# Routing tokens to experts: three fixed slots per expert and a table for the rest, in place of one table for all

## The chip, the core and the metric

The kernel runs on one core of one Trainium2 chip. A core has five engines with queues of their own: TensorE (PE, with its weight loads shown apart as PEld), VectorE (DVE), ScalarE (ACT), GpSimd (POOL) and SyncE (SP, which here only issues transfers). Sixteen DMA engines serve transfers that SP or POOL issue. The metric is the time of one execution on the device in microseconds (us), lower is better; kernels are compared by the median of their runs.

## The reference

Chunked attention over q, k, v of shape 4 x 8 x 768 x 64, with eight memory rows per head, gives 3072 tokens of 512 values. These go through a mixture of experts:

```python
h_dense = np.maximum(x @ w1_dense, 0.0)
y_dense = h_dense @ w2_dense
logits = x @ w_gate
expert_idx = np.argmax(logits, axis=1)
...
for e in range(E):
    mask = expert_idx == e
    h = np.maximum(x[mask] @ w1[e], 0.0)
    y_moe[mask] = gate_w[mask, None] * (h @ w2[e])
return (y_dense + y_moe).astype(np.float32)
```

There are E = 8 experts with weights of 512 x 512, twice each. `gate_w` is the softmax weight of the chosen expert. The inputs are drawn with a fixed seed, so how many tokens go to which expert is the same in every run: 339, 581, 96, 448, 352, 375, 288 and 593 for experts 0 to 7 (worked out by running the reference's attention and gate on its inputs).

## The kernel before, in words

**Attention stage.** The 3072 tokens are 24 tiles of 128. A loop written out by hand (`manual_schedule`, so the order of the code is the order on each engine) runs iterations 0 to 28, and in each of them different parts of several tiles: scores of tile i, values of tile i-2, the transposes of tile i-3, the gate of tile i-4, the dense first layer of tile i-7 (L363, its Relu in L365). SP issues the value windows (`load_v`, L182) and the gate's weights (`wgate`, L444, after the second window). POOL issues q and k (`load_qk`) and the expert weights (`load_w`, L83), one half of one expert at a time: 12 halves in the iterations of `W_AT`, one behind the loop, four more around the first slots. All weights end in one SBUF tile `wall`. Constants are set in iteration 0, among them a row `zrow` (L114 to L117) that says "no token".

**Routing.** Every third tile, `choose`, `rank` and `place` (DVE and PE) give each token of three tiles a row in a DRAM buffer `xs`, which has a region of 3072 rows per expert. `scatter` (L424, an indirect DMA of POOL) writes each token's row there: its values in bf16, its dense hidden values, its gate weight and its number. At the end `cnt` (L526) holds the tokens per expert.

**Table.** From `cnt`, some twenty small DVE operations (L541 to L582) build a table of 31 slots: for slot j its expert (`expi`) and the 128 row numbers of `xs` (`rowi`; lanes without a token point at the zero row).

**Slots.** Each slot handles 128 rows of one expert. `fetch` (L594) gathers the rows by an indirect DMA of POOL, `turn` (L602) transposes them on PE and copies the result out (half on DVE, half on ACT), `bring` (L612) reads the expert's number into a DVE register and copies that expert's weights out of `wall` by two DVE copies, `first` (L623) is the first layer (16 matmuls, L628), `second` (L634) the dense and the expert's second layer (four matmuls each), `send` (L646) scales on ACT and `put` (L655) stores by an indirect DMA of POOL to the tokens' rows of the output. `run` interleaves them: in slot n it brings slot n+1, runs its own first layer, the dense second layer, turns slot n+1, runs its own second layer, sends, and fetches four slots ahead. Slots 0 to 26 always run; four further slots run inside an If (L698) when the table has more than NSURE = 27 slots. Their fetches, and their stores of a zeroed tile, run in any case.

Of the kernel before, what the change touches and what calls it, by code (L numbers as in the profile page):

```python
# [17 lines left out]
ENGINES = [mybir.EngineType.PE, mybir.EngineType.DVE, mybir.EngineType.Activation]  # L18
# [17 lines left out]
NSLOT = NT + E - 1  # L36
NSURE = 27
NSPLIT = 20
XW = DM // 2
ROW = 2 * XW + 2  # L40
ZROW = E * CAP
NOWHERE = 1 << 20
GRP = 3
QKB = 5
NVB = 4
W_AT = (10, 13, 15, 16, 18, 19, 21, 22, 24, 25, 26, 27)
NXG = 5
# [3 lines left out]
def kernel(  # L51
# [19 lines left out]
    xs = nc.dram_tensor("xs", [E * CAP + 1, ROW], I32, kind="Internal").ap()  # L71
# [14 lines left out]
    w_todo = [(E, 1)] + [(e, half) for e in range(E) for half in range(2)]  # L86
# [12 lines left out]
    zrow = const.tile([1, ROW], F32, name="zrow")  # L99
    rowi = const.tile([128, NSLOT], I32, name="rowi")  # L100
    expi = const.tile([128, NSLOT], I32, name="expi")
    nsl = const.tile([128, 1], I32, name="nsl")
    thr_i = const.tile([128, NT], I32, name="thr_i")
    thr = const.tile([128, NT], F32, name="thr")
    lane_i = const.tile([128, 1], I32, name="lane_i")
    lane = const.tile([128, 1], F32, name="lane")
    slot_i = const.tile([128, NSLOT], I32, name="slot_i")
    slot = const.tile([128, NSLOT], F32, name="slot")
    low = const.tile([128, E, E], F32, name="low")

    def constants():
        nc.vector.memset(ones, 1.0)
        nc.vector.memset(oh_sum, 0.0)
        nc.vector.memset(zrow, 0.0)  # L114
        nc.vector.memset(zrow[:, ROW - 2:ROW - 1], 1.0)
        nc.vector.memset(zrow[:, ROW - 1:ROW].bitcast(I32), NOWHERE)
        nc.sync.dma_start(xs[ZROW:ZROW + 1, :], zrow.bitcast(I32))  # L117
        for e in range(E):
            nc.gpsimd.memset(prio[:, e:e + 1], float(E - e))
            nc.gpsimd.memset(ecap[:, :, e:e + 1], float(e * CAP // 128))  # L120
        nc.gpsimd.iota(tok, [[128, NT]], base=0, channel_multiplier=1)
        nc.gpsimd.affine_select(upper, ones, pattern=[[1, 128]], base=0,
                                channel_multiplier=-1, compare_op=ALU.is_gt, fill=0.0)

    def table_constants():
        nc.gpsimd.iota(thr_i, [[128, NT]], base=0, channel_multiplier=0)
        nc.gpsimd.iota(lane_i, [[0, 1]], base=0, channel_multiplier=1)
        nc.gpsimd.iota(slot_i, [[1, NSLOT]], base=0, channel_multiplier=0)
        nc.vector.tensor_copy(thr, thr_i)
        nc.vector.tensor_copy(lane, lane_i)  # L130
        nc.vector.tensor_copy(slot, slot_i)
        nc.vector.memset(low, 0.0)
# [3 lines left out]
    with ExitStack() as one:  # L136
# [4 lines left out]
        small = one.enter_context(tc.tile_pool(name="small", bufs=2))  # L141
        ps = one.enter_context(tc.tile_pool(name="ps", bufs=4, space=PSUM))
        px = one.enter_context(tc.tile_pool(name="px", bufs=1, space=PSUM))
        pf = one.enter_context(tc.tile_pool(name="pf", bufs=1, space=PSUM))
# [25 lines left out]
        vebuf = [c1.tile([128, HP, D + 1], F32, name=f"ve{n}") for n in range(2)]  # L170
        vws = {n: vbuf[n % NVB] for n in range(B * NP)}
        ves = {b: vebuf[b % 2] for b in range(B)}
# [102 lines left out]
        def attention(g, qT, kbd):  # L275
# [84 lines left out]
            def dense():  # L360
                ph = pf.tile([128, F], F32, tag="ph", name="ph")
                for d in range(DT):
                    nc.tensor.matmul(ph, st["xT"][:, d, :], wall[:, E, d, :],  # L363
                                     start=(d == 0), stop=(d == DT - 1))
                nc.scalar.activation(st["row"][:, XW:2 * XW].bitcast(BF16), ph, AF.Relu,  # L365
                                     scale=st["grp"]["gt"][:, st["u"], 0:1])

            return {"scores": scores, "exp": expo, "turn": turn, "values": values, "norm": norm,
                    "keep_x": keep_x, "turn_x": turn_x, "gate": gate, "dense": dense}

        scatters = []

        def wide(ap, n=GRP):
            return ap.unsqueeze(2).to_broadcast([128, n, E])

        def choose(grp):
            lg = grp["pg"]
            mx = small.tile([128, GRP], F32, tag="gmx", name="gmx")
            nc.vector.reduce_max(mx, lg, axis=AX.X)
            df = small.tile([128, GRP, E], F32, tag="df", name="df")  # L380
            nc.vector.tensor_tensor(df, lg, wide(mx), ALU.subtract)
            pr = small.tile([128, GRP, E], F32, tag="pr", name="pr")
            nc.vector.scalar_tensor_tensor(
                pr, df, 0.0, prio.unsqueeze(1).to_broadcast([128, GRP, E]),
                op0=ALU.is_ge, op1=ALU.mult)
            pm = small.tile([128, GRP], F32, tag="pm", name="pm")
            nc.vector.reduce_max(pm, pr, axis=AX.X)
            oh = small.tile([128, GRP, E], BF16, tag="oh", name="oh")
            nc.vector.tensor_tensor(oh, pr, wide(pm), ALU.is_equal)
            ex = small.tile([128, GRP, E], F32, tag="ex", name="ex")  # L390
# [3 lines left out]
        def weigh(grp):  # L394
            nc.vector.reduce_sum(grp["gt"][:, :, 0], grp["ex"], axis=AX.X)

        def rank(grp, last):
            oh = grp["oh"]
            rk = ps.tile([128, GRP, E], F32, tag="ps", name="rk")
            nc.tensor.matmul(rk, ones, ecap, start=True, stop=False)  # L400
            for t in range(GRP):
                nc.tensor.matmul(rk, ones, oh_sum[:, t:t + 1, :].to_broadcast([128, GRP, E]),
                                 start=False, stop=False)
            for t in range(GRP - 1):
                nc.tensor.matmul(rk[:, t + 1:, :], ones,
                                 oh[:, t:t + 1, :].to_broadcast([128, GRP - 1 - t, E]),
                                 start=False, stop=False)
            nc.tensor.matmul(rk, upper, oh, start=False, stop=True)
            (nc.vector if last else nc.gpsimd).tensor_tensor(oh_sum, oh_sum, oh, ALU.add)
            grp["rk"] = rk  # L410

        def place(grp):
            at = small.tile([128, GRP, E], F32, tag="at", name="at")
            nc.vector.tensor_tensor(at, grp["rk"], grp["oh"], ALU.mult)
            si = small.tile([128, GRP], I32, tag="si", name="si")
# [3 lines left out]

        def scatter(g):  # L420
            st = tiles.pop(g)
            grp, u, row = st["grp"], st["u"], st["row"]
            nc.gpsimd.tensor_copy(row[:, ROW - 2:], grp["gt"][:, u, :])  # L423
            i = nc.gpsimd.indirect_dma_start(  # L424
                xs[:, :], bass.IndirectOffsetOnAxis(ap=grp["si"][:, u:u + 1], axis=0),
                row.bitcast(I32), None, bounds_check=E * CAP - 1, oob_is_err=False)
            for o in scatters:
# [14 lines left out]
        make_identity(nc, identf)  # L442
        load_v(1)
        nc.sync.dma_start(wgate, moe_w_gate.rearrange("(t p) m -> p t m", p=128))  # L444
# [10 lines left out]
        parts, grps = {}, {}  # L455
        LAG_X, LAG_G, LAG_D = 3, 4, 7
        for i in range(NT + LAG_G + 1):
# [4 lines left out]
            if i < NT:  # L462
# [9 lines left out]
                if i % GRP == 0:  # L472
                    grps[i // GRP] = {}
                tiles[i]["grp"], tiles[i]["u"] = grps[i // GRP], i % GRP
            gg = i - LAG_G
            grp = grps[gg // GRP] if 0 <= gg < NT else None
            last = grp is not None and gg % GRP == GRP - 1
# [4 lines left out]
            if i == 2:  # L482
                load_w(E, 0)
                table_constants()
            if i in W_AT:
                next_w()
            if i % 2 == 0:
                load_v(i // 2 + 2)
            if grp is not None and gg % GRP == 0:
                grp["pg"] = pg.tile([128, GRP, E], F32, tag="pg", name="pg")  # L490
                grp["gt"] = small.tile([128, GRP, 2], F32, tag="gt", name="gt", bufs=3)
                nc.gpsimd.tensor_copy(grp["gt"][:, :, 1].bitcast(I32), tok[:, gg:gg + GRP])
# [8 lines left out]
            if i < NT + LAG_G:  # L501
                do("dense", LAG_D)
            else:
                for g in range(i - LAG_D, NT):
                    parts[g]["dense"]()
            do("gate", LAG_G)
# [9 lines left out]
            if last:  # L516
# [6 lines left out]
                weigh(grp)  # L523
                place(grp)
# [4 lines left out]
            if i >= LAG_D:  # L529
                scatter(i - LAG_D)  # L530
        for g in range(NT + LAG_G + 1 - LAG_D, NT):
            scatter(g)
        next_w()
# [6 lines left out]
        m24 = wide_t[1][:, :E * NT].rearrange("p (e t) -> p e t", t=NT)  # L540
        nc.vector.tensor_tensor(m24, cnt.unsqueeze(2).to_broadcast([128, E, NT]),  # L541
# [196 lines left out]
```

## Time and profile before

| what | value |
|---|---|
| median of three runs | 290.79 us (288.57 to 292.19) |
| the profiled execution, its own time | 287.78 us |
| its span, first to last instruction | 286.1 us |
| granted TensorE clock, mean | 0.921 |
| busy share: PE, DVE, ACT, POOL | 77%, 60%, 49%, 67% |
| DMA, mean over the span | 45.15 MB, 158 GB/s |
| idle of PE ahead of the turns, waiting for fetched rows | 25.6 us |

The profile comes from one execution. Times in it are microseconds from the span's start unless marked ns. A group's row gives line, engine, operation, output<-inputs and shape, then the count, busy time and mean duration of one in ns, and behind the second bar the idle time of the engine just before these instructions with what ended it. A row of the timeline gives start, duration, engine, line and count, and in brackets the idle before it. A row of the windows gives, for a stretch of time, the busy time of each engine, the granted clock, the DMA engines' busy share (which can pass 1 where packets overlap) and GB/s.

### The profile page before, as it was taken

Reading aid. Unit: us, or ns where it says so; the run is one execution under the profiler, and the core shown is the slowest. Engines: PE = TensorE matmul, PEld = TensorE weight load, DVE = VectorE, ACT = ScalarE, POOL = GpSimd, SP = SyncE. Lnnn points to the kernel's source line nnn. Section 1 sums busy time; section 2 is a strip of 40 time slices with the busy share of each in tenths; the row PEclk is TensorE's granted clock in tenths of the full one; section 3 lists DMA queues with packets and bytes.
Section 4 is the critical chain, followed back from the end, with each engine's and each line's share of the span. In section 5 each row is a group of like instructions: output and inputs, shape, how many; then the busy total and the mean of one; then the engine's idle time right before and its main releaser. Section 6 shows DMA issues by size and latency. Waiting matters only on the chain. (4 is left out here: it accounts for less than half of the span.)

```text
span 286.1 us, 9435 instructions
## 1 busy us (share of the span) xinstructions
PE 219.7 (77%) x3770; PEld 163.6 (57%) x3804; DVE 173.0 (60%) x384; ACT 140.9 (49%) x230; POOL 190.5 (67%) x274
## 2 busy tenths in 40 slices
PE   2435759999879969998997202997999999865691
PEld 1324658877767857867775002664666667534460
DVE  5586356888768967988974711464556656552230
ACT  2434446776976767653553200353546656441341
POOL 8864034599958984885879807365676877887732
PEclk9999977999999997999999855797999999995979
DMA  6999546599998999699969995994455555454231
GB/s 88 179 200 172 109 84 93 101 174 166 170 234 134 212 218 221 96 210 223 200 129 177 204 165 123 193 230 141 139 158 158 183 153 173 152 162 131 84 112 60
DMA packets 54368, 45.15 MB, mean 158 GB/s; under 512 B 30319, under 2 KB 49263, under 8 KB 54322
## 3 DMA queue, kind: packets, MB, share of 16 engines
q0 software_dynamic: 25376, 36.54, 62.1%
q1 hardware_dynamic: 28946, 7.98, 15.2%
q8 instruction: 31, 0.51, 0.8%
q14 instruction: 15, 0.12, 0.1%
HBM read 46.05 MB, written 14.44 MB: 211 GB/s over the span
## 5 line engine op out<-in xcount | busy, mean ns | idle before, releaser
L596 POOL DMA_INDIRECT xg<-xs,rowi x31 | 36.6, 1180 | 24.3 <-issue 13.1
L609 ACT COPY xT<-xt 128x512 bf16<-128x512 bf16 x27 | 15.8, 586 | 59.9 <-DVE xT L608 59.9
L608 DVE COPY xT<-xt 128x512 bf16<-128x512 bf16 x27 | 11.5, 425 | 50.6 <-PE xt L606 50.6
L656 POOL DMA_INDIRECT out_dram<-o,xg x27 | 28.1, 1039 | 18.7 <-ACT o L651 9.0
L606 PE MATMUL xt<-ident,xg 128*128 128x128 bf16 x216 | 18.2, 233 | 25.6 <-DMA xg<-xs,rowi 25.6
L628 PEld LDWEIGHTS <-wa 128*128 128x128 bf16 x432 | 29.2, 105 | 9.0 <-issue 2.3
L606 PEld LDWEIGHTS <-xg 128*128 128x128 bf16 x216 | 15.0, 104 | 33.8 <-DMA xg<-xs,rowi 29.4
L424 POOL DMA_INDIRECT xs<-row,si x24 | 29.6, 1233 | 6.8 <-POOL row L423 6.5
L628 PE MATMUL ph<-xT,wa 128*128 128x128 bf16 x432 | 31.5, 231 | 1.5 <-ACTq L698 1.0
L351 POOL CAST xT<-x 128x512 bf16<-128x512 f32 x24 | 15.0, 626 | 25.0 <-ACT x L349 21.7
L643 PE MATMUL py<-wb,h 128*128 128x512 bf16 x108 | 30.8, 412 | 0.0
L357 PEld LDWEIGHTS pg<-wgate,x 128*128 128x128 f32 x192 | 26.1, 199 | 5.9 <-ACT qT L257 2.4
L322 PE MATMUL xp<-vw,aT 64*32 64x65 f32 x1536 | 25.6, 233 | 4.9 <-DMA vw<-mtpl 3.0
L223 DVE COPY vw<-vw 24x1820 f32<-24x1820 f32 x24 | 27.5, 1147 | 2.5 <-DMA vw<-in_v_dram 1.8
L363 PE MATMUL ph<-wall,xT 128*128 128x512 bf16 x76 | 23.5, 390 | 5.8 <-issue 2.1
L341 POOL CAST row<-xn 128x512 bf16<-128x512 f32 x24 | 19.5, 814 | 11.6 <-DVE xn L334 11.4
L617 DVE COPY wa<-wall 128x2048 bf16 (+1 forms) x27 | 20.4, 755 | 11.3 <-DVE gw L648 7.6
L305 ACT ACTIVATE a<-a 128x512 f32<-128x512 f32 x24 | 15.1, 630 | 24.0 <-DVE a L300 22.5
L640 PE MATMUL py<-wall,xT 128*128 128x512 bf16 x94 | 25.6, 388 | 0.9 <-issue 0.2
L357 PE MATMUL pg<-wgate,x 128*128 128x8 f32 x192 | 24.4, 253 | 2.3 <-DMA wgate<-in_moe_w_gate_dram 2.3
L322 PEld LDWEIGHTS xp<-vw,aT 64*32 64x32 f32 x1536 | 19.2, 109 | 11.7 <-issue 5.6
L265 ACT COPY kbd<-tp 64x768 bf16<-64x768 bf16 x28 | 22.1, 790 | 3.4 <-PE tp L252 3.2
(122 smaller groups left out, 449.4 us busy)
## 6 DMA issues: line engine op xcount, KB each, us to landing
wall<-in_moe_w_dram POOLq DMA_DIRECT2D x16, 512.0 KB, 9.2
vw<-in_v_dram SPq DMA_DIRECT2D x64, 64.0 KB
kb<-in_k_dram POOLq DMA_DIRECT2D x16, 192.0 KB, 6.0
qb<-in_q_dram POOLq DMA_DIRECT2D x16, 192.0 KB, 6.9
vw<-in_v_dram SPq DMA_DIRECT2D x32, 56.0 KB
vw<-mtpl SPq DMA_DIRECT2D x24, 65.0 KB
wall<-in_moe_w_dense_dram POOLq DMA_DIRECT2D x2, 512.0 KB, 8.5
xg<-xs,rowi POOLq DMA_INDIRECT x31, 4.2
```

The lines of the kernel that those rows point to most:

```text
L223: nc.vector.tensor_copy(vw[r + 32:r + 56, :PC - 1], vw[r:r + 24, 1:])
L265: nc.scalar.copy(dst, tv[r])
L322: nc.tensor.matmul(xp[32 * cc:32 * cc + 32, par, (D + 1) * hp:(D + 1) * (hp + 1)], st["aT"][r, hp, 32 * cc:32 * cc + 32], vw[r, 4 * (g % 2 ...
L357: nc.tensor.matmul(grp["pg"][:, u, :], st["x32"][:, d, :], wgate[:, d, :], start=(d == 0), stop=(d == DT - 1))
L363: nc.tensor.matmul(ph, st["xT"][:, d, :], wall[:, E, d, :], start=(d == 0), stop=(d == DT - 1))
L424: i = nc.gpsimd.indirect_dma_start(xs[:, :], bass.IndirectOffsetOnAxis(ap=grp["si"][:, u:u + 1], axis=0), row.bitcast(I32), None, bounds_c ...
L596: nc.gpsimd.indirect_dma_start(xg.bitcast(I32), None, xs[:, :], bass.IndirectOffsetOnAxis(ap=rowi[:, j:j + 1], axis=0), bounds_check=ZROW, ...
L606: nc.tensor.transpose(xt[:, d, :], xb[:, 128 * d:128 * d + 128], ident)
L628: nc.tensor.matmul(ph[:, f, :], w[:, d, 128 * f:128 * f + 128], xT[:, d, :], start=(d == 0), stop=(d == DT - 1))
L640: nc.tensor.matmul(py, xts[j][:, DT + f, :], wall[:, E, DT + f, :], start=(f == 0), stop=False)
L643: nc.tensor.matmul(py, hs[j][:, f, :], copied[j][1][:, f, :], start=False, stop=(f == FT - 1))
L656: i = nc.gpsimd.indirect_dma_start(out[:, :], bass.IndirectOffsetOnAxis(ap=xgs.pop(j)[:, ROW - 1:ROW].bitcast(I32), axis=0), o, None, boun ...
```

## The change

Every expert gets three fixed slots (FIX = 3, 24 in all, slots 0 to 23); slot j uses expert j // 3, with its weights read in `wall` where they lie. Tokens beyond 384 of an expert go to table slots: three of these (SURE = 3, slots 24 to 26) run always, the other 18 (slots 27 to 44) in an If that is entered when the table needs more than three. Table slots still copy their weights. A slot's 128 rows are now contiguous in `xs`: each region of `xs` starts with 128 filler rows, and a slot that is not full ends at the expert's last row, so that it also reads rows of the slot before, or filler. A lane that is not the slot's own is masked by `past`, which sends its store out of range. SP reads the start row into a register and issues a plain DMA.

Weights: expert 0, the dense second layer and expert 1 are loaded in the attention stage (iterations 12, 15, 17, 19, 21), the other twelve halves in the slots of `W_SLOT`. The attention loop has one iteration less; the last dense tiles run behind the last gate, in other PSUM buffers. Value windows have five buffers and are loaded one window further ahead; `wgate` goes ahead of the second window. Eight transfers of SP write the filler rows (`front`). 36 matmuls whose result is not used stand ahead of the first turn.

```diff
-NSLOT = NT + E - 1
-NSURE = 27
-NSPLIT = 20
+FIX = 3
+NFIX = FIX * E
+NOVER = NT - FIX
+SURE = 3
+REG = CAP + 128
...
-QKB = 5
-NVB = 4
-W_AT = (10, 13, 15, 16, 18, 19, 21, 22, 24, 25, 26, 27)
-NXG = 5
+GROUPS = [GRP] * 7 + [2, 1]
+QKB = 4
+NVB = 5
+W_AT = (12, 15, 17, 19, 21)
+W_SLOT = (0, 1, 3, 4, 6, 7, 9, 10, 12, 13, 15, 16)
+NXG = 6
+NIDLE = 36
...
-    w_todo = [(E, 1)] + [(e, half) for e in range(E) for half in range(2)]
+    w_todo = [(0, 0), (0, 1), (E, 1)] + [(e, half) for e in range(1, E) for half in range(2)]
...
-        nc.vector.memset(zrow, 0.0)
...
-        nc.sync.dma_start(xs[ZROW:ZROW + 1, :], zrow.bitcast(I32))
+        nc.vector.memset(wall[:, E - 1], 1.0)
...
+    def front(e):
+        i = nc.sync.dma_start(
+            xs[REG * e:REG * e + 128, :],
+            wall[:, E - 1].rearrange("p t m -> p (t m)")[:, :2 * ROW].bitcast(I32))
...
+        nc.sync.dma_start(wgate, moe_w_gate.rearrange("(t p) m -> p t m", p=128))
         load_v(1)
-        nc.sync.dma_start(wgate, moe_w_gate.rearrange("(t p) m -> p t m", p=128))
...
+        send_at = {i: [i - 7] for i in range(7, 25)}
+        send_at.update({25: [18], 26: [19, 20], 27: [21]})
+        dense_at = {i: [i - 7] for i in range(7, 25)}
+        dense_at.update({25: [18, 19], 26: [20], 27: [21, 22, 23]})
...
-            if i % 2 == 0:
-                load_v(i // 2 + 2)
+            if 3 <= i < 3 + E:
+                front(i - 3)
+            if i < 2:
+                load_v(i + 2)
+            elif i % 2 == 0:
+                load_v(i // 2 + 3)
...
+        rs = tmp(FS, "rsf")
+        nc.vector.tensor_tensor(rs, full, cnt.unsqueeze(2).to_broadcast(FS), ALU.min)
+        nc.vector.tensor_tensor(by_slot(rowi), rs, base, ALU.add)
+        nc.vector.tensor_tensor(rs, full, rs, ALU.subtract)
+        nc.vector.tensor_scalar(by_slot(past), rs, lane, float(NOWHERE),
+                                op0=ALU.is_gt, op1=ALU.mult)
...
         def fetch(j):
-            xg = w3.tile([128, ROW], F32, tag="xg" + own[0], name="xg", bufs=NXG)
-            nc.gpsimd.indirect_dma_start(
-                xg.bitcast(I32), None, xs[:, :],
-                bass.IndirectOffsetOnAxis(ap=rowi[:, j:j + 1], axis=0),
-                bounds_check=ZROW, oob_is_err=True)
+            at = nc.sync.value_load(rowi[:1, j:j + 1], min_val=0, max_val=E * REG - 128)
+            xg = w3.tile([128, ROW], F32, tag="xg", name="xg", bufs=NXG)
+            nc.sync.dma_start(xg.bitcast(I32), xs[bass.ds(at, 128), :])
...
         def bring(j):
+            if j < NFIX:
+                w = wall[:, j // FIX]
+                was[j] = w[:, :DT], w[:, DT:]
+                return
+            k = j - NFIX
+            ev = nc.vector.value_load(expi[:1, k:k + 1], min_val=0, max_val=E - 1)
...
+            to = w3.tile([128, 1], I32, tag="to", name="to")
+            nc.vector.tensor_scalar(to, xg[:, ROW - 1:ROW].bitcast(I32), past[:, j:j + 1],
+                                    float(NOWHERE), op0=ALU.max, op1=ALU.min)
...
+        sure = list(range(NFIX + SURE))
+        more = list(range(NFIX + SURE, NSLOT))
+        for j in sure[:NXG]:
             fetch(j)
         bring(0)
+        idle = pf.tile([128, DM], F32, tag="py", name="idle")
+        for n in range(NIDLE):
+            nc.tensor.matmul(idle, ident, wall[:, E, n % DT], start=True, stop=True)
         turn(0)
...
+        run(sure)
+        count = nc.values_load(nov[:1, :1], min_val=0, max_val=NOVER)
+        with tc.If(count > SURE, preferred_fallthrough_block=False):
+            for j in more[:NXG]:
+                fetch(j)
             bring(more[0])
             turn(more[0])
+            run(more)
```

In `run`, the fetch now goes NXG = 6 slots ahead, and nothing outside the given list of slots is brought, turned or fetched.

289 lines of the change are left out of this document (146 added, 143 removed).

## The prediction

> **What bounds the kernel now.** I read the windows by stage first, then the timeline of the slots for their pace, then the groups by line and the waits for the stalls in them. The attention stage ends near 163 us; a gap without TensorE work follows; from 176 us on the routed tiles ("slots") run.
>
> ```profile
> 163.00:178.00 15.00, 1.20 (x10) 0.93 (x11) 1.90 (x4) 0.14 (x1) 5.63 (x7) 0.50 0.77 155
> 176.20:183.35 7.15, 6.33 (x39) 4.41 (x41) 2.94 (x6) 1.75 (x3) 3.81 (x5) 0.53 0.90 187
> 183.35:192.34 8.99, 8.94 (x96) 6.20 (x96) 5.46 (x12) 4.85 (x9) 5.04 (x5) 1.00 1.16 217
> 192.34:198.94 6.60, 4.56 (x33) 2.67 (x33) 2.59 (x7) 2.36 (x4) 3.13 (x4) 0.82 0.49 137
> 198.94:246.74 47.80, 46.46 (x474) 32.05 (x480) 26.94 (x61) 27.29 (x46) 35.81 (x32) 0.99 0.53 165
> ```
>
> Columns: stretch, length, busy time of PE, PEld, DVE, ACT, POOL, granted clock, DMA share, GB/s. In the fifth row PE is busy 46.46 of 47.80 us at clock 0.99: an undisturbed slot is TensorE-bound. Its pace, from the output copies (eleven slots apart), and the number of slots:
>
> ```profile
> 212.22 0.69 ACT L651 ACTIVATE o<-py,gw 128x512 f32<-128x512 f32 x1
> 245.95 0.69 ACT L651 ACTIVATE o<-py,gw 128x512 f32<-128x512 f32 x1
> L628 PE MATMUL ph<-xT,wa 128*128 128x128 bf16 x432 | 31.5, 231 | 1.5 <-ACTq L698 1.0 <-DVE xT L608 0.5
> ```
>
> 33.73 / 11 = 3.07 us a slot, and 432 matmuls of 16 a slot are 27 slots: the four spare ones in the If of before are skipped. From the first of these matmuls (177.84) to the last of the span (280.12) are 102.3 us; 27 x 3.07 is 82.9. The other 19.4 are a cold start and late fetches:
>
> ```profile
> 177.84 1.89 PE L628 MATMUL ph<-xT,wa 128*128 128x128 bf16 x16 [0.52 <-DVE xT L608]
> 183.35 1.06 PE L628 MATMUL ph<-xT,wa 128*128 128x128 bf16 x16
> 196.46 0.98 PE L606 MATMUL xt<-ident,xg 128*128 128x128 bf16 x8 [1.99 <-DMA xg<-xs,rowi]
> 260.50 1.03 PE L606 MATMUL xt<-ident,xg 128*128 128x128 bf16 x8 [5.71 <-DMA xg<-xs,rowi]
> 271.23 0.69 PE L606 MATMUL xt<-ident,xg 128*128 128x128 bf16 x8 [2.36 <-DMA xg<-xs,rowi]
> 279.08 1.04 PE L643 MATMUL py<-wb,h 128*128 128x512 bf16 x4
> L596 POOL DMA_INDIRECT xg<-xs,rowi x31 | 36.6, 1180 | 24.3 <-issue 13.1 <-PE ph L628 3.5 <-DMA out_dram<-o,xg 2.9
> L656 POOL DMA_INDIRECT out_dram<-o,xg x27 | 28.1, 1039 | 18.7 <-ACT o L651 9.0 <-issue 8.2 <-DMA out_dram<-o,xg 1.2
> ```
>
> The first slot takes 183.35 - 177.84 = 5.5 us, 2.4 over pace; the other 17.0 come with fetches that POOL issues one behind the other with the stores (1.18 and 1.04 us each).
>
> **The change, part by part.**
>
> *How many slots run.* This decides the sign. The reference's seeded draw sends 339, 581, 96, 448, 352, 375, 288 and 593 tokens to the eight experts (worked out from the reference; their rounded-up tiles are 3+5+1+4+3+3+3+5 = 27, the number in the row of L628). Three fixed slots an expert are 24, of which experts 2's second and third are empty. Beyond 384 tokens lie 2, 1 and 2 tiles of experts 1, 3 and 7: five. SURE is 3, so `count > SURE` holds, and the If then runs all of `more`, slots 27 to 44: 18 slots, of which 2 hold tokens. So 45 slots run, not 27. An empty slot fetches 128 rows, transposes and multiplies them like a full one; only its store writes nothing. 18 x 3.07 = **+55.3**. The pace could be set by another engine there, since these slots copy their weights on VectorE:
>
> From the waits, and the groups by line:
>
> ```profile
> DVE wa L617 <- DVE gw L648: 7.6, 21, 0.7
> ```
>
> ```profile
> L617 DVE COPY wa<-wall 128x2048 bf16 (+1 forms) x27 | 20.4, 755 | 11.3 <-DVE gw L648 7.6
> L619 DVE COPY wb<-wall 128x2048 bf16 x26 | 19.7, 757 | 0.3
> L608 DVE COPY xT<-xt 128x512 bf16<-128x512 bf16 x27 | 11.5, 425 | 50.6 <-PE xt L606 50.6
> L648 DVE RECIPROCAL gw<-xg 128x1 f32<-128x1 f32 x27 | 4.0, 153 | 0.0
> ```
>
> 0.76 + 0.76 + 0.43 + 0.15, a new clamp like the reciprocal (0.15) and a register load (0.36, the idle ahead of a copy: 7.6 / 21) are 2.6 us, under 3.07; POOL keeps only the store. Pace between 3.07 and, with a half microsecond of late weights, 3.4 (+6): 3.07.
>
> *Entering the If.* Nearest row, in the timeline, is the If of before whose body was skipped; beside it the row of the queue that brings instructions:
>
> ```profile
> 246.74 1.05 PE L628 MATMUL ph<-xT,wa 128*128 128x128 bf16 x16 [0.97 <-ACTq L698]
> q8 instruction: 31, 0.51, 0.8%
> ```
>
> 0.97 us of PE, and there the next tile was already turned. Now slot 26 ends without the next turn under its Relu (0.4 more), and slot 27's xT copy (0.43) stands open: **+1.9**. SP has six buffers and passes the branch some six slots earlier, so its fetches are ready. Bounds: 1, and 6 if SP or DVE come late. By the row of queue 8 a block of instructions (0.51 MB / 31 = 16 KB) took 0.8% x 286.1 x 16 / 31 = 1.2 us; one such block for PE and one for DVE in line would make 4.
> The Trainium skill, "Runtime: NRT & Kernel Launch", Instruction fetch mechanics, speaks against this: a taken branch whose target lies outside the two loaded pages must first fetch its page. By it the entry is nearer 4 than 1.9 and the sum 2 us higher; the row of 0.97 does not show whether its own jump paid this.
>
> *Weights in place.* Fixed slots copy no weights: DVE is relieved of 1.5 us a slot, which lay beside 3.07 us of PE: nothing.
>
> *Fetch by SP.* POOL keeps 1.04 + 0.3 us a slot, SP fetches six ahead; the 17.0 us of late fetches go: **-17.0**. Bounds: -17 and -8, if half of them are slow transfers. Next late would be the weights.
>
> *Weight loads in the slots.* Twelve of seventeen loads move to slots 0 to 16. Timeline and DMA issues (KB each, us to landing):
>
> ```profile
> 177.85 2.46 POOL L83 DMA_DIRECT2D wall<-in_moe_w_dram  x3
> 186.97 0.83 POOL L83 DMA_DIRECT2D wall<-in_moe_w_dram  x1
> wall<-in_moe_w_dram POOLq DMA_DIRECT2D x16, 512.0 KB, 9.2
> out_dram<-o,xg POOLq DMA_INDIRECT x27, 3.2
> ```
>
> Fetch and store cost 0.53 x 47.80 / 15.6 slots = 1.63 us of the sixteen engines. From 176.20 to 198.94 the shares sum to 0.90 x 7.15 + 1.16 x 8.99 + 0.49 x 6.60 = 20.1 us; about 7.5 fetches and stores take 6.1, four loads the rest: 3.5 each. Slots 0 to 16 then ask for 12 x 3.5 + 17 x 1.63 = 70 us in 52; at the highest share seen (1.16) they need 60. A load has at least five slots (15 us) against a landing of 9.2, and slots 18 to 26 drain the excess; but stores queue behind loads on POOL's queue and the o buffers are three. Between 0 and +8: **+2**, since a landing of 3.2 plus one load still fits in two slots.
>
> *The tail of attention and the gap.* Timeline, and the landing of the row scatters:
>
> ```profile
> 152.48 1.03 PE L363 MATMUL ph<-wall,xT 128*128 128x512 bf16 x4
> 153.37 1.06 PE L357 MATMUL pg<-wgate,x 128*128 128x8 f32 x8
> 154.47 0.18 DVE L379 TENSOR_REDUCE gmx<-pg 128x3 f32<-128x24 f32 x1 [3.03 <-PE pg L357]
> 156.32 0.15 DVE L526 COPY cnt<-cp 128x8 f32<-128x8 f32 x1
> 162.55 0.98 POOL L424 DMA_INDIRECT xs<-row,si  x1 [0.28 <-POOL row L423]
> 172.80 1.10 POOL L596 DMA_INDIRECT xg<-xs,rowi  x1 [8.46 <-issue]
> 176.29 1.03 PE L606 MATMUL xt<-ident,xg 128*128 128x128 bf16 x8 [15.54 <-DMA xg<-xs,rowi]
> xs<-row,si POOLq DMA_INDIRECT x24, 6.2
> ```
>
> The last gate stays near 154.4 (one dense more ahead of it); three denses follow (3.1), then rank, place, the last Relu and label (about 2): last scatter near 160.4, two us earlier. No load is in flight, so it lands in the median 6.2 where the wait of before lasted until 172.80. The fixed row numbers need four DVE operations, not twenty: hidden. 166.6 plus a fetch (3.2; before 176.29 - 172.80 = 3.5 with POOL's generation) is 169.8: **-6.5**, between -9 and -2.
>
> *36 idle matmuls.* Four take 1.03 us, spaced 0.21: 7.7 us, from about 159 to 167, ahead of the first rows: no cost. They leave under 3 us of pause: first slot warm, **-2.4** (bounds -2.4, 0).
> The Trainium skill, "TensorE: Matmul & The Clock Gate", What's actually happening, has the array fall to half rate after an idle window of about 3.4 us. The trace agrees (1.89 us, then 1.06, for the same sixteen); by the rule a pause of 4 us would give the 2.4 back.
>
> *Early attention.* Timeline, and groups by line and shape:
>
> ```profile
> 40.71 1.85 PE L357 MATMUL pg<-wgate,x 128*128 128x8 f32 x8 [2.28 <-DMA wgate<-in_moe_w_gate_dram]
> L439 DVE MEMSET kbd<- 128x3168 uint32 x1 | 2.7, 2698 | 0.6 <-issue 0.6
> L114 DVE MEMSET zrow<- 1x514 f32 x1 | 0.5, 487 | 0.0
> ```
>
> wgate one window earlier: **-2.3**. The fill of wall's last expert (2048 words by L439's 0.85 ns: 1.7) replaces zrow's 0.6 ahead of the first maximum: **+1.1**. Eight front writes (0.8 us of SP each) sit behind value windows that are prefetched one further: 0, at worst +5. Seven fewer load issues on POOL in that stage: hidden, at best -3.
>
> **Sum** on the profiled execution (287.8 us; its span 286.1): 287.8 + 55.3 + 1.9 - 17.0 + 2.0 - 6.5 - 2.4 - 2.3 + 1.1 = 319.9. The median shown, 290.8, is 3.0 above the profiled execution; its spread comes mostly with fetch stalls that go, so I add 1: **321**.
>
> **Rivals.** (1) *The If is skipped* (at most three tiles over 384, or the reference's draw not the one run): 321 - 57.2 = 264, faster. It decides between 3 and 4 tiles; the draw has five, and the 27 slots of the trace agree with it. 0.03. Cheap empty slots would need 1.6 us a slot for a draw; PE's 3.07 excludes it. (2) *DMA-bound slots 0 to 16*: the row of 1.16 speaks for it, the slack of five slots against: +6, 327. 0.15. (3) *A slow If*: code pages, late fetches or 3.4 a slot: 327. 0.14. The branch rule of the Trainium skill above belongs here. (4) *Late fetches stay*, being slow transfers: +8, 329; the issue waits of POOL speak against. 0.10. My sum: 0.58.
>
> **How the numbers follow.** The likeliest case alone reaches from 314 to 326. Low, over all: 321 with the other ends of attention (-3), gap (-2.5), load cost (-2), entry (-0.9) and without the 1 for the runs: 311. High: two of rivals 2 to 4 together, 6 + 8, and 1 for the runs: 336. Outside lie rival 1 and about 0.12 of worse or better sums. Two per cent is about what a measurement of this kernel can tell from no change. Faster 0.03 (rival 1), same 0.01, slower 0.96.
>
> **What would show it.** 45 x 16 = 720 matmuls at the first-layer line; 45 stores; 18 pairs of weight copies; a pace of 3.07 before and in the If; slot 0's sixteen matmuls in 1.06 us; first turn near 170. Waits of ACT's o on stores in slots 0 to 16 mean rival 2; a pause over 3 us at the If, rival 3; 432 matmuls, rival 1, and the prediction is wrong.

## The result, and the profile after

The changed kernel takes 327.16 us (median of four runs, 323.69 to 329.54) where the kernel before took 291.49 us on the same chip (288.57 to 294.45). The ratio is 1.117, with a 95% interval of 1.105 to 1.128: slower, as forecast. The prediction was 321 us with a range of 311 to 336; 321 / 290.79 is 1.104, just under the interval. The executions of the changed kernel fall into two groups, 323.7 to 324.9 us and 329.4 to 329.5 us, and the profiled one (329.41 us, span 327.7) is of the longer group, so part of what follows in the attention stage belongs to that one execution.

First the windows by stage of the changed kernel (columns as in the prediction): part of attention, the gap, slots 0 to 16, and 18 slots in the If.

```profile
60.00:105.00 45.00, 35.35 (x882) 27.75 (x880) 29.98 (x61) 26.70 (x45) 30.00 (x49) 0.94 1.07 208
163.40:178.80 15.40, 13.99 (x75) 6.85 (x74) 8.02 (x39) 2.19 (x5) 7.49 (x15) 0.89 0.38 123
178.79:229.00 50.21, 48.62 (x509) 33.64 (x509) 9.89 (x45) 27.79 (x47) 22.65 (x26) 1.00 1.08 248
264.00:320.00 56.00, 55.19 (x572) 37.68 (x569) 33.04 (x88) 32.06 (x55) 20.70 (x18) 1.00 0.27 75
```

In the last row TensorE is busy for 55.19 of 56.00 us at full clock, VectorE for 33.04 only: the slots in the If are TensorE-bound, empty or not. Their number stands in the groups by line and shape:

```profile
L718 POOL DMA_INDIRECT out_dram<-o,to x45 | 48.4, 1076 | 84.9 <-ACT o L717 74.1 <-DVE wab L682 9.7 <-DVE xT L669 1.1
L691 PE MATMUL ph<-xT,wall 128*128 128x128 bf16 x384 | 25.4, 219 | 0.6 <-DVE xT L669 0.6
L691 PE MATMUL ph<-xT,wab 128*128 128x128 bf16 x336 | 22.2, 219 | 0.6 <-DVE xT L669 0.6
```

384 / 16 = 24 slots read `wall` in place, 336 / 16 = 21 use copied weights; 45 stores. (The prediction's sign of 18 pairs of weight copies left out the three table slots that always run: there are 21.) The pace is read from the Relu of each slot in the timeline (slots 0, 26, 27 and 44):

```profile
179.88 0.60 ACT L694 ACTIVATE h<-ph 128x512 bf16<-128x512 f32 x1 [0.52 <-PE ph L691]
262.06 0.60 ACT L694 ACTIVATE h<-ph 128x512 bf16<-128x512 f32 x1
265.94 0.60 ACT L694 ACTIVATE h<-ph 128x512 bf16<-128x512 f32 x1 [0.58 <-PE ph L691]
318.07 0.60 ACT L694 ACTIVATE h<-ph 128x512 bf16<-128x512 f32 x1
```

In the If: (318.07 - 265.94) / 17 = 3.066 us a slot. Entering it: 265.94 - 262.06 = 3.88, 0.81 over pace. Now the rows around the gap, from TensorE's timeline: the last gate, the idle matmuls, the first turn, and the first layers of slots 0 and 1.

```profile
163.31 1.18 PE L377 MATMUL pg<-wgate,x 128*128 128x8 f32 x8
169.78 7.93 PE L749 MATMUL idle<-wall,ident 128*128 128x512 bf16 x36 [0.62 <-ACT row L389]
177.60 0.62 PE L667 MATMUL xt<-ident,xg 128*128 128x128 bf16 x8
178.79 1.05 PE L691 MATMUL ph<-xT,wall 128*128 128x128 bf16 x16 [0.57 <-DVE xT L669]
181.85 1.06 PE L691 MATMUL ph<-xT,wall 128*128 128x128 bf16 x16
```

The last gate starts at 163.31, 9.9 us later than before (153.37), and the first turn at 177.60, 1.3 us later (176.29): attention became slower, the gap shorter. The place of the attention loss shows in VectorE's timeline as the steps between the score maxima (L318, one per tile):

```profile
91.75 0.69 DVE L318 TENSOR_REDUCE mx<-sc 128x8 f32<-128x512 f32 x1
103.64 1.10 DVE L243 COPY vw<-vw 24x1820 f32<-24x1820 f32 x1 [9.50 <-DMA vw<-mtpl]
106.78 0.68 DVE L318 TENSOR_REDUCE mx<-sc 128x8 f32<-128x512 f32 x1
```

One tile took 106.78 - 91.75 = 15.0 us, since a value window had not landed; in before the 23 steps average 5.3. The chain of waits through that stretch, and SP's timeline of issues there, name what was ahead of the window:

```profile
80.74 5.76 DMA ve<-in_v_dram
86.52 10.91 DMA xs<-wall
97.49 7.99 DMA vw<-in_v_dram
```

```profile
84.23 1.45 SPq L229 DMA_DIRECT2D vw<-mtpl  x2
85.72 2.94 SPq L134 DMA_DIRECT2D xs<-wall  x2
88.77 9.03 SPq L220 DMA_DIRECT2D vw<-in_v_dram  x8
98.61 2.48 SPq L229 DMA_DIRECT2D vw<-mtpl  x2
```

Two filler writes (`xs<-wall`, L134) go out at 85.72; the eight window issues behind them take 9.03 us (such a set took 5.6 to 8.5 in before), and the chain follows a filler write for 10.91 us. The stall also costs clock: from 100 to 107.5 us, while TensorE waits for the window and just after, its granted clock is 0.50. Later in that execution TensorE idles again (2.26 us at 138, for nothing that the profile shows), and then runs at half clock for the fourteen microseconds of this window, although it is never idle in them. That this second stretch comes of the windows is not shown.

```profile
140.00:154.00 14.00, 14.00 (x211) 10.63 (x211) 9.67 (x15) 5.47 (x9) 7.88 (x11) 0.51 0.16 49
```

### The profile page after: what moved, and what is told of

Same layout as the page of the kernel before. It is cut to its first block, busy times and chain, and to the rows that moved or that the text cites. A ratio compares the mean times of both kernels' runs of the same rounds, so it can differ in the third digit from the quotient of the medians.

```text
span 327.7 us, 11139 instructions
## 1 busy us (share of the span) xinstructions
PE 282.1 (86%) x4420; PEld 203.6 (62%) x4420; DVE 182.9 (56%) x467; ACT 172.4 (53%) x285; POOL 166.0 (51%) x258
## 4 chain that ended last, share of the span: by engine, by line
PE 62%; DMA 24%; issue 4%; POOL 3%; DVE 2%; SPq 2%; ACT 1%; POOLq 0%; DVEq 0%; ACTq 0%
PE ph L691 10%; PE py L706 9%; PE py L703 9%; DMA out_dram<-o,to 8%; PE ph L384 6%; PE xp L342 5%; DMA vw<-in_v_dram 5%; PE pg L377 5%; PE xt L667 4%; DMA vw<-mtpl 3%; DMA xs<-wall 3%; PE xtp L367 3%; PE ap L330 3%; PE idle L749 2%; PE tp L272 2%
## 5 line engine op out<-in xcount | busy, mean ns | idle before, releaser
L718 POOL DMA_INDIRECT out_dram<-o,to x45 | 48.4, 1076 | 84.9 <-ACT o L717 74.1
L670 ACT COPY xT<-xt 128x512 bf16<-128x512 bf16 x45 | 26.4, 586 | 56.2 <-DVE xT L669 47.2
L703 PE MATMUL py<-wall,xT 128*128 128x512 bf16 x180 | 46.2, 379 | 0.0
L342 PE MATMUL xp<-vw,aT 64*32 64x65 f32 x1536 | 26.5, 243 | 14.3 <-DVE vw L246 11.0
L717 ACT ACTIVATE o<-py,gw 128x512 f32<-128x512 f32 x45 | 31.2, 693 | 8.8 <-DMA out_dram<-o,to 5.3
L682 DVE COPY wab<-wall 128x2048 bf16 x42 | 27.2, 691 | 8.4 <-PE py L706 5.9
L694 ACT ACTIVATE h<-ph 128x512 bf16<-128x512 f32 x45 | 26.8, 596 | 5.6 <-PE ph L691 1.9
L691 PEld LDWEIGHTS <-wall 128*128 128x128 bf16 x384 | 23.5, 98 | 6.1 <-issue 0.7
L706 PE MATMUL py<-wall,h 128*128 128x512 bf16 x96 | 24.7, 379 | 1.9 <-ACT h L694 1.9
L691 PE MATMUL ph<-xT,wall 128*128 128x128 bf16 x384 | 25.4, 219 | 0.6 <-DVE xT L669 0.6
L330 PE MATMUL ap<-identf,a 128*128 128x128 f32 x96 | 17.5, 312 | 7.8 <-ACT a L325 7.8
```

What stands on the lines that cost most here:

```text
L330: nc.tensor.transpose(ap[:, hp, :], st["a"][:, 2 * hp:2 * hp + 2, :], identf)
L342: nc.tensor.matmul(xp[32 * cc:32 * cc + 32, par, (D + 1) * hp:(D + 1) * (hp + 1)], st["aT"][r, hp, 32 * cc:32 * cc + 32], vw[r, 4 * (g % 2 ...
L682: nc.vector.tensor_copy(wab[:, r], wall[:, :E][:, bass.ds(ev, 1), r].rearrange("p a t m -> p (a t) m"))
L691: nc.tensor.matmul(ph[:, f, :], w[:, d, 128 * f:128 * f + 128], xT[:, d, :], start=(d == 0), stop=(d == DT - 1))
L703: nc.tensor.matmul(py, xts[j][:, DT + f, :], wall[:, E, DT + f, :], start=(f == 0), stop=False)
L706: nc.tensor.matmul(py, hs[j][:, f, :], was[j][1][:, f, :], start=False, stop=(f == FT - 1))
```

## The experiments

Every run was compared with the kernel before on its own chip (its medians there were 289.5 to 290.3 us); ratios are to that. Several of the kernels have only slots 27 and 28 in the If ("If of two"): they leave out the table slots past the 29th, which hold no token in this draw.

### Are the empty slots the loss?

Five sure slots: the If holds sixteen slots and is not entered, 29 run.

```diff
-SURE = 3
+SURE = 5
```

> SURE is 5 instead of 3: 29 slots run and the If is not entered. If the time is the number of slots (3.07 us each, full or empty), 16 slots fewer take 49.1 us off the changed kernel's 324.5, and the cost of entering and leaving the If (2 to 4 us) goes too: 272 us, range 268 to 277, with 29 x 16 = 464 first-layer matmuls. If empty slots were nearly free and the loss lay elsewhere (in the attention stage, in the weight loads), it stays above 290.

Measured: 280.51 us (275.62 to 284.73) against 289.52 for the kernel before, which is a ratio of 0.969 of the medians, without an interval. The direction is as expected, but it is 8 us over the 272 that was expected and outside 268 to 277. And the If entered, but with two slots:

```diff
-        more = list(range(NFIX + SURE, NSLOT))
+        more = list(range(NFIX + SURE, NFIX + 5))
```

> The If is entered as in the changed kernel, but holds two slots instead of 18 (27 and 28, the only ones with tokens): the same 29 slots as with SURE = 5, plus the If. Cheap If, as in my sum: 1 to 2 us over the kernel with SURE = 5. Slow If (rival 3): 4 to 6 us over it. The profile of the changed kernel shows 0.8 us lost on TensorE on the way in, and 2 us more than before between the last copy and the end of the span; if that is the way out, the difference is about 3.

Measured: 275.24 us, ratio 0.958 (0.944 to 0.973). Both theories had it slower than five sure slots; it is 5 us faster. The step into the If is the same as with eighteen slots, from the Relus of slots 26 to 28:

```profile
257.25 0.60 ACT L694 ACTIVATE h<-ph 128x512 bf16<-128x512 f32 x1
261.12 0.60 ACT L694 ACTIVATE h<-ph 128x512 bf16<-128x512 f32 x1 [0.58 <-PE ph L691]
264.18 0.60 ACT L694 ACTIVATE h<-ph 128x512 bf16<-128x512 f32 x1
```

3.87, then 3.06. So the sixteen empty slots alone turn the sign: without them the changed kernel is faster than the one before. Against the 52 us between 327.2 and 275.2 (different chips; 49 from the middle of the shorter executions, 324.6) stand 16 x 3.066 = 49.1. That skipping is dearer than entering shows at the end of the two spans: with five sure slots the last output copy ends at 268.0 and the span at 277.5, 9.5 us; with the If of two 266.6 and 272.5, 5.9 us. In the first, the record of TensorE's compare-and-branch at the If lasts 3.65 us, and POOL's closing work starts about 0.1 us behind its end; in the second, as in the changed kernel, it lasts 0.22 us. The Trainium skill, "Runtime: NRT & Kernel Launch", Instruction fetch mechanics, says that a taken branch whose target is not in the two loaded pages waits for its page to be fetched. The rows fit that, but in the other direction than the prediction used it for: the long record is the one that jumps over the body. That it is the fetch of a page is not shown.

### Do the filler writes delay the value windows?

The eight filler writes behind most of the window loads, with all 45 slots:

```diff
-            if 3 <= i < 3 + E:
-                front(i - 3)
+            if 17 <= i < 17 + E:
+                front(i - 17)
```

> All 45 slots as in the changed kernel, but the eight filler writes are issued in iterations 17 to 24, behind the last value window on SP's queue, instead of 3 to 10. If they are what holds up the value windows (the stall of 15 us near 92 us in the changed kernel's profile), 4 to 10 us go: 315 to 320. If the stall comes from the weight loads or from the value windows themselves, or was one execution's, no change within 1 us: 323 to 326. If late fillers delay the first fetch, up to 4 us more.

Measured: 320.57 us, ratio 1.113 (1.095 to 1.130), not to be told from the changed kernel's 1.117. The same with SURE = 5:

> SURE = 5 and the late filler writes together. If both theories hold the gains add: 272 less 4 to 10 is 262 to 268. If the filler writes are innocent: as with SURE = 5 alone, 272.

Measured: 275.2 us, ratio 0.956 (0.940 to 0.972): over the 272 that both theories allowed at most, and 5.3 us under five sure slots with early fillers, whose own runs lie 9 us apart. These two with late fillers are on one chip: 45.4 us for sixteen slots less the dearer skip. Then on one chip the If of two again, and the If of two with late fillers:

> The kernel with an If of two slots once more, as the base of the three that follow on the same chip: 275 us, within 2.

Measured: 273.5 us, ratio 0.948 (0.934 to 0.962).

> The base with the eight filler writes in iterations 17 to 24. If they hold up the value windows, the step of 9 to 15 us between two tiles near 93 us goes from the profile and the time falls by 3 to 6 us. If that step is only moved (the same writes held up something else at 124 us in the 45-slot kernel), by 0 to 2. If they are innocent, no change.

Measured: 272.26 us, ratio 0.949 (0.939 to 0.959). That the fillers delay the windows is shown, what it costs is not. VectorE's waits on window transfers between 60 and 150 us sum to 12.9 us in the changed kernel, 8.7 and 3.7 in the first two experiments, 9.0 in the first one of this pair, and to nothing in the three kernels with late fillers (before: 0.5). Windows of the pair, early fillers first:

```profile
60.00:105.00 45.00, 39.12 (x1016) 31.23 (x1001) 33.95 (x71) 29.34 (x50) 32.07 (x52) 0.95 1.09 217
```

```profile
60.00:105.00 45.00, 42.87 (x1042) 34.24 (x1030) 38.03 (x79) 33.10 (x56) 35.67 (x58) 0.96 1.01 186
```

TensorE and VectorE do some 4 us more work there with the fillers gone. But the last gate came at 155.6 with early fillers and 156.8 with late ones, because with late ones a step of 8.1 us followed at 127, where TensorE waited 2.4 us for nothing that the profile shows (before has one of 7.0 at 126.3). What that step is stays open. And in the profile of five sure slots with late fillers, where no window was late either, the last gate came only at 167.0, with a granted clock of 0.50 from 145 to 155 us. A kernel without filler writes was not tried, since its slots would read rows that nothing wrote.

### Is it SP's own queue that stops the late fetches?

The start row and the fetch on POOL's queue, six ahead as on SP, with the If of two:

```diff
-            at = nc.sync.value_load(rowi[:1, j:j + 1], ...
+            at = nc.gpsimd.value_load(rowi[:1, j:j + 1], ...
...
-            nc.sync.dma_start(xg.bitcast(I32), xs[bass.ds(at, 128), :])
+            nc.gpsimd.dma_start(xg.bitcast(I32), xs[bass.ds(at, 128), :])
```

> The base with the row fetches issued by POOL again (register load and plain transfer on POOL's queue, still six slots ahead). If the late fetches of the kernel before came from POOL's order of fetch and store, POOL has about 1.3 us of store, 1.2 of fetch and 0.6 of weight load a slot in slots 0 to 16, more than the pace of 3.07: turns wait for rows again and it is 3 to 10 us slower. If they were slow transfers, or are cured by fetching further ahead, 0 to 1 us.

Measured: 285.19 us, ratio 0.988 (0.975 to 1.001), 11.7 us above the If of two beside it. By the two profiles 8.2 of it are the steps around the If (7.82 and 1.17 us over pace for slots 27 and 28, in place of 0.84 and nothing) and 2.2 POOL's closing drain (7.2 us in place of 5.0). (In these two profiles the last gates lie 5.0 us apart as well, ahead of any fetch.) TensorE's and POOL's timelines at the If:

```profile
260.64 1.04 PE L706 MATMUL py<-wab,h 128*128 128x512 bf16 x4
267.32 1.03 PE L667 MATMUL xt<-ident,xg 128*128 128x128 bf16 x8 [5.64 <-DMA xg<-xs]
268.92 1.86 PE L691 MATMUL ph<-xT,wab 128*128 128x128 bf16 x16 [0.57 <-DVE xT L669]
```

```profile
262.68 0.98 POOL L718 DMA_INDIRECT out_dram<-o,to  x1 [1.04 <-ACT o L717]
264.32 0.58 POOL L660 DMA_DIRECT2D xg<-xs  x1 [0.66 <-issue]
```

POOL passes the branch only behind its last store (262.68), so slot 27's fetch goes out at 264.32, and the array is cold besides (1.86 for sixteen matmuls). SP had passed the branch long before (16 us ahead of TensorE in the If of two): its queue is worth some 8 us at the If. Ahead of the If, though, no turn waited for a fetch on POOL either. So sharing a queue with the stores does not by itself make fetches late. Of before's 17 us, 12 lie in the turns from 260.50 on, behind POOL's extra work for the spare tiles (fetches, memsets and stores around 247 to 266), 3.8 at the turn of 196.46, and 1.1 are before's own If. Which of that extra work, the shorter distance of four and the dearer indirect fetch (1.18 us of POOL; 0.56 for the plain one here) makes them late was not taken apart.

### What are the weight loads worth, here and there?

Twelve loads back in attention, five in the slots, fillers early, If of two, on the chip of the pair above:

```diff
-W_AT = (12, 15, 17, 19, 21)
-W_SLOT = (0, 1, 3, 4, 6, 7, 9, 10, 12, 13, 15, 16)
+W_AT = (10, 12, 13, 15, 16, 18, 19, 21, 22, 24, 25, 26)
+W_SLOT = (0, 3, 6, 9, 12)
```

> The base with seven of the twelve weight loads moved back from the slots into the attention stage (twelve there, five in slots 0, 3, 6, 9, 12). If the slots lose their 3 us to loads that stand ahead of the stores, the steps over 3.3 us in slots 0 to 20 mostly go: slots 2 us shorter; the attention stage pays for seven loads of 3.5 us of DMA each, 0 to 5 us. Net -2 to +3. If the steps have another cause, the slots stay as they are.

Measured: 284.54 us, ratio 0.985 (0.976 to 0.995), 11 us above the If of two. In the slots the steps over pace sum to 1.0 us in place of 2.8, of which 0.8 is the If: the loads there cost 1.8. In attention the last gate moved from 155.6 to 169.8. So, by the medians, taking seven loads out of attention is worth some 13 us there while the fillers are in it, and it costs 2 in the slots. Part of the 13 can be clock (0.87 from 60 to 150 us, against 0.96). The reverse, the five remaining loads later:

```diff
-W_AT = (12, 15, 17, 19, 21)
+W_AT = (20, 21, 23, 24, 26)
```

> Edit: the five expert-weight loads of the attention stage go in iterations 20, 21, 23, 24, 26 in place of 12, 15, 17, 19, 21; fillers stay early; two slots in the If (table slots past the 29th left out, empty in this draw). Base: f0_base29, ratio 0.948, 12.1 us step between two score tiles at 93.0 us, last gate at 156.4, first turn 169.6. Theory A (attention is bounded by the DMA engines between 60 and 105 us, where f0 moved 9.78 MB with all sixteen busy; two loads of 0.51 MB are 10 % of it): the step at 93 falls from 12.1 to about 8, last gate 3 to 4 us earlier, ratio about 0.937, unless the late loads hold up the rows after the last scatter. Theory B (the value windows are late by their own order on SP and their five buffers, whatever else is on the engines): the step at 93 stays at 10 to 13 and the ratio at 0.948 within a per cent.

Measured: 276.54 us, ratio 0.940 (0.930 to 0.951). The step at 91 us is still 12.0 and VectorE still waits 7.0 us for windows: the forecast of about 8 from less traffic was wrong, and theory B's 10 to 13 held. From 60 to 105 us the DMA share is down to 0.96 here, from 1.09; with the fillers where they are, two loads fewer do not help. Then loads and fillers late:

```diff
-W_AT = (12, 15, 17, 19, 21)
+W_AT = (20, 21, 23, 24, 26)
...
-            if 3 <= i < 3 + E:
-                front(i - 3)
+            if 19 <= i < 19 + E:
+                front(i - 19)
```

> Edit: as k1_base29_loads_late, and the eight filler writes (2.06 MB) in iterations 19 to 26, behind the last value window. So of the 9.78 MB between 60 and 105 us 3.1 MB are gone. Theory A: no step over 7 us after 60 us, last gate near 149, gate to first turn perhaps a few us longer as the fillers and the last loads land among the last scatters; ratio 0.92 to 0.935. Theory B: a step of 8 us or more stays, wherever the windows are late, and the ratio stays at 0.948 within a per cent. If the late transfers hold up the first rows, the first turn is no earlier than 168 although the gate is.

Measured: 275.12 us against 289.87, a ratio of 0.949 of the medians, without an interval. In its windows the DMA engines are down to 0.92 in this stretch, and VectorE gets 5.0 us more done than in the If of two (38.91 against 33.95):

```profile
60.00:105.00 45.00, 42.90 (x1102) 35.60 (x1110) 38.91 (x82) 35.61 (x60) 37.53 (x58) 1.00 0.92 173
```

No step over 6 us is left between 60 and 120, the last gate comes at 152.0, 3.6 us before that of the If of two, and yet the time is not shorter: the first turn is at 168.25, as the expectation's last sentence had it. The gain is given back behind the gate, as the two profiles show: gate to first turn 16.2 us in place of 14.0 (fillers and loads are still landing: DMA share 0.80 from 150 to 160, where the other has 0.24), and 3.5 us more over pace in the slots, 1.6 of them a cold first slot (below). The version that leaves nothing out, with SURE = 5:

> Edit: the changed kernel whole, with SURE = 5 (the If holds sixteen slots and is not entered in this draw), and loads and fillers late as in k2_base29_both_late. Nothing is left out of the computation. Theory A: e4_both's 0.956 less what k2 gains over f0 (0.013 to 0.028): 0.93 to 0.943; the skipped If still costs about 4 us at the end beside k2. Theory B: 0.956 within a per cent.

Measured: 277.09 us, ratio 0.959 (0.951 to 0.966); its last gate is at 151.9. Theory B's 0.956 within a per cent held in time. Like the two kernels of SURE = 5 above, it computes everything and is faster than before, by some 4%, and 50 us under the changed kernel (another chip).

### Do the idle matmuls do anything?

```diff
-        for n in range(NIDLE):
+        for n in range(1):
```

> Edit: one idle matmul in place of 36 ahead of the first turn; two slots in the If; everything else as f0_base29 (so its attention stage is a second look at f0's). If the idle matmuls keep the clock up: the first slot's sixteen first-layer matmuls take about 1.9 us in place of 1.05, the step of the first slot is some 1.6 to 2.4 us over pace, and the ratio rises by 0.006 to 0.008 over f0's 0.948. If the eight transposes of the first turn and what comes before them are enough: 1.05 us and the same ratio. The pause of TensorE ahead of the first turn is about 13 us without them.

Measured: 276.55 us, ratio 0.943 (0.934 to 0.952), no different from 0.948 in time. The timeline shows their effect all the same: first turn, and the sixteen first-layer matmuls of slot 0, without them, then in the If of two, and then in the two kernels with loads and fillers late (If of two, five sure):

```profile
179.69 1.03 PE L667 MATMUL xt<-ident,xg 128*128 128x128 bf16 x8 [8.62 <-DMA xg<-xs]
181.29 1.86 PE L691 MATMUL ph<-xT,wall 128*128 128x128 bf16 x16 [0.57 <-DVE xT L669]
```

```profile
169.63 0.62 PE L667 MATMUL xt<-ident,xg 128*128 128x128 bf16 x8 [1.28 <-DMA xg<-xs]
170.83 1.05 PE L691 MATMUL ph<-xT,wall 128*128 128x128 bf16 x16 [0.57 <-DVE xT L669]
```

```profile
168.25 1.03 PE L667 MATMUL xt<-ident,xg 128*128 128x128 bf16 x8 [3.50 <-DMA xg<-xs]
169.86 1.86 PE L691 MATMUL ph<-xT,wall 128*128 128x128 bf16 x16 [0.57 <-DVE xT L669]
```

```profile
168.60 0.62 PE L667 MATMUL xt<-ident,xg 128*128 128x128 bf16 x8 [2.22 <-DMA xg<-xs]
169.79 1.24 PE L691 MATMUL ph<-xT,wall 128*128 128x128 bf16 x16 [0.57 <-DVE xT L669]
```

Pauses of 1.28, 2.22, 3.50 and 8.62 us ahead of the turn go with 1.05, 1.24, 1.86 and 1.86 us. But the pause does not settle it alone. With five sure slots and early fillers a pause of 1.60 us gave a turn at full rate and then this:

```profile
174.72 1.71 PE L691 MATMUL ph<-xT,wall 128*128 128x128 bf16 x16 [0.57 <-DVE xT L669]
179.44 1.06 PE L691 MATMUL ph<-xT,wall 128*128 128x128 bf16 x16
```

Here, and behind the pause of 2.22, the clock fell during slot 0, and the slot took 4.72 us, as long as without idle matmuls (4.70); behind 1.91 us, in the run with POOL's fetch, it took 3.06. A cold start costs 1.64 from the first to the second slot's first layer and 0.40 in the turn, 2.0 in all without idle matmuls, which is less than the runs scatter. The Trainium skill, "TensorE: Matmul & The Clock Gate", What's actually happening, puts the fall to half rate after an idle window of about 3.4 us. The pauses of 3.50 and 8.62 agree; that the clock also fell behind 1.60 and 2.22, and not behind 1.91, a limit on this pause alone does not give.

## Why the prediction was right in sign and a little short

The steps of the sum, on the profiled executions (287.8 before, 329.4 after):

| step | predicted | measured | from |
|---|---|---|---|
| 18 more slots | +55.3 | +55.2 | 18 x 3.066 |
| entering the If | +1.9 | +0.8 | 3.88 - 3.07 |
| late fetches | -17.0 | -17.3 | steps over pace, before (its own If, 1.1, among them) |
| weight loads in the slots | +2.0 | +2.5 | steps over pace, after, without the If |
| first slot warm | -2.4 | -2.4 | 5.51 to 3.06, slot 0 to slot 1 |
| attention to the last gate | -0.2 | +9.9 | 153.37 to 163.31; forecast 154.4 - 2.3 + 1.1 = 153.2 |
| last gate to first turn | -7.5 | -8.6 | 22.9 to 14.3; forecast 169.8 - 154.4 = 15.4 |
| last output copy to the end | 0 | +2.0 | 5.2 to 7.2 |
| sum | +32.1 | +42.1 | 287.8 + 42.1 = 329.9, against 329.4 |

*How many slots run* was right to a tenth, and it decides everything: 45 slots, the empty ones at the full pace. *Late fetches* was right in size; its reason, POOL's one queue for fetches and stores, was not enough by itself to make fetches late in the run with POOL's fetch, except at the If. *Entering the If* was high by 1.1 (its own terms add up to 1.8, not 1.9): SP's rows were ready, and TensorE's branch took 0.23 us. *Weight loads* was right, mechanism too; from the waits of the changed kernel:

```profile
ACT o L717 <- DMA out_dram<-o,to: 5.3, 7, 1.9
```

Seven output copies wait 5.3 us together for a store to free their buffer, and the slow slots are 5, 8, 14, 17 and 20. The rival of DMA-bound slots named this wait, but at +6 where it is 2.5.

The step that failed is the one on early attention: "Eight front writes (0.8 us of SP each) sit behind value windows that are prefetched one further: 0, at worst +5." That put the term at nothing although its stretch had no room. The rows that spoke against it were at hand, in the windows and in SP's timeline of the kernel before:

```profile
60.00:105.00 45.00, 40.80 (x1048) 33.50 (x1034) 36.95 (x79) 32.78 (x55) 38.53 (x62) 1.00 1.07 187
```

```profile
84.45 6.37 SPq L200 DMA_DIRECT2D vw<-in_v_dram  x8
90.86 1.44 SPq L209 DMA_DIRECT2D vw<-mtpl  x2
92.41 8.21 SPq L200 DMA_DIRECT2D vw<-in_v_dram  x8
```

From 60 to 105 us the DMA engines' share is 1.07 already, and SP's issues follow one another almost without a gap: their records fill 44.2 of the 45 us. The fillers add eight times 257 KB, 2.06 MB, to the 8.4 MB moved there, and in the changed kernel their issues take 7.75 us of SP. At the 187 GB/s of that row the bytes alone would be 11 us of the engines, but this is an estimate from the high side: with the fillers in it, the If of two moved 217 GB/s at a share of 1.09. The Trainium skill, "DMA: Bandwidth & Descriptors", Issuing engines are not separate DMA queues, says that transfers run on the same sixteen engines and interleave, whoever issued them. No run here separates that from the order on SP's own queue; the run with the five loads later, where the share was 0.96 and the windows were 7.0 us late all the same, speaks rather for SP's queue. "Seven fewer load issues ... hidden, at best -3" was off the other way, by the run that puts them back: some 13 us with the fillers there. What it would be without the fillers was not tried.

How much of the 9.9 us the late windows make is open. The profiles, with VectorE's waits for windows and the granted clock from 60 to 150 us:

| kernels | waits for windows, us | clock | last gate, us |
|---|---|---|---|
| before | 0.5 | 0.98 | 153.4 |
| fillers early: changed, five sure, If of two (twice), POOL's fetch, one idle matmul | 12.9, 8.7, 3.7, 9.0, 0.5, 7.8 | 0.89, 0.91, 0.89, 0.96, 0.95, 0.83 | 163.3, 159.2, 159.0, 155.6, 160.6, 165.9 |
| fillers early, twelve loads in attention | 12.1 | 0.87 | 169.8 |
| fillers early, five loads late | 7.0 | 0.92 | 157.2 |
| fillers late: 45 slots, five sure, If of two | 0, 0, 0 | 0.94, 0.86, 0.96 | 155.6, 167.0, 156.8 |
| both late: If of two, five sure | 0, 0 | 0.94, 0.96 | 152.0, 151.9 |

That the fillers delay the windows is shown: five of the six kernels with this attention stage unchanged wait 3.7 to 12.9 us, and the five with late fillers do not wait at all. The last gate, though, goes with the granted clock at least as closely as with these waits, and it was low (0.86) in one profile where no window was late; a low clock can follow a stall, but need not. Moving the fillers made no kernel measurably faster. The middle of the six, 159.9, is 6.7 us over the 153.2 of the prediction; with the gap (-1.1), the If (-1.1) and the end (+2.0) that makes 6.5, about the distance between 321 and 327, but the six lie 10 us apart, so this is no proof. That 327 is near the price of rivals 2 and 3 is luck: neither made the difference.

The two sized terms of early attention did not both come true. TensorE no longer waits for `wgate`. The fill of wall's last expert was priced at 1.7 us and took 3.47, and the first score maximum came at 21.73 instead of 19.43, 2.3 later where the sum had 1.1:

```profile
17.97 3.47 DVE L122 MEMSET wall<- 128x4096 bf16 x1 [0.80 <-issue]
```

*The gap* closed by 1.1 more than forecast: from the last scatter (170.87) to the first turn it took 6.7 us, where the sum had 6.2 for the landing and 3.2 for a fetch, while the last scatter came 7.6 us behind the last gate, where the sum had 6.0. The first turn itself came at 177.60, not near 170, since the gate was late. *The end* was not in the sum: POOL's closing drain took 6.35 us, in before 3.2.

## What to carry to other kernels

Count how many iterations a fixed layout runs before weighing what each of them saves: here 16 empty slots at 3.07 us buried some 15 us of real gains. Price an added transfer by what is left in its own stretch, on the queue that issues it and on the DMA engines; where neither has room, as from 60 to 105 us here, something else will be late. And a transfer moved out of a full stretch is paid where it lands: look at the rows behind it before counting the gain.

## What the runs showed of the hardware that was not expected

- A conditional body that is skipped can cost more than one that is entered: TensorE's compare-and-branch lasted 3.55 to 3.75 us over a body of sixteen slots (three kernels), 0.36 over before's four (whose If lacks `preferred_fallthrough_block=False`, so length is not the only difference), and 0.22 to 0.23 where the body was entered.
- POOL's drain at the end took 3.2 us after before's 31 stores, 6.35 after 45, and after 29 stores 5.0 in most kernels, 5.7 with five loads in the slots, 7.2 with the fetches on POOL and 3.9 with the If skipped. What sets it was not tried.
- After an idle of 2.26 us TensorE was granted 0.51 of its clock for fourteen microseconds in which it never idled (140 to 154 in the changed kernel), and after one of 1.57 us 0.50 from 145 to 155 with five sure slots and late fillers; in the second profile of the If of two, with the changed kernel's attention stage, the clock from 140 to 150 was 1.00.
